# Throwaway products, a permuted identity, first-column steps and a new hand-written order in a fused FFT and state-space kernel

## The chip, the cores and the metric

The kernel runs on one core of one Trainium2 chip. The core has five engines that run their own instruction queues side by side: TensorE (PE in the profile, with its weight loads as PEld), VectorE (DVE), ScalarE (ACT), GpSimd (POOL) and SyncE (SP, which only starts transfers here). The metric is the device time in microseconds (us) of one execution, lower is better. The kernel before takes 306.85 us, the median of three runs that lie between 306.59 and 307.20 us.

## The reference

Two long computations on the same input x of 2048 tokens by 1024 channels (bf16) are blended by a gate:

```python
x = A_x
g = _sigmoid((x * gate_w).sum(-1, keepdims=True))
a = irfft2(rfft2(x) * (w_r + 1j * w_i))            # over tokens and channels
# b: a diagonal complex recurrence over the tokens
Lam_bar = exp(dt * Lam);  B_bar = ((Lam_bar - 1) / Lam)[:, None] * Bmat
Bu = einsum("bld,pd->blp", x, B_bar)
h = Lam_bar * h + Bu[:, t]                          # for t in 2048 tokens
b = 2 * einsum("blp,dp->bld", hseq, Cmat).real + x * Dskip
return g * a + (1 - g) * b
```

## The kernel before

**Spectral half.** Both directions of the two-dimensional transform are matrix products with constant tables. The 2048 tokens are taken as 16 groups j of 128. `turn` (L932) transposes a group on TensorE by eight products of 128 columns with the permuted identity `ident_g`, and `turn_out` (L941) copies the result to `xQ`; groups 12 to 15 come transposed by DMA. `fold` (L951) makes even and odd parts on VectorE, for the last groups with a mirrored half (`mirror`, `fold_odd`). `fd` (L432) is the first transform on TensorE, `fd_out` (L458) evicts it on ScalarE, `s1` and `s1_out` (L466, L478) are the first half of the token transform, which is stored to DRAM. `s2` (L602) is the second half, `times_w` (L628) multiplies by the weights on VectorE (tile `UV`), `is1`, `is2` (L640, L673) and `spectral_mm` (L819) go back.

**First column.** Column 0 of the spectrum packs two real columns and has its own small chain, `middle` (L533): a reversal of a weight tile (`Wrev`), a combination on GpSimd (`Wh`, `AB`), a small transform (`Bcol`, `Zp`), its reversal (`Zr`), a complex product (`Q`, `Qb`) and a permutation (`qps`, `Qn`). Its small TensorE products stand in the one TensorE queue between large ones; `Qn` overwrites column 0 of the tile `X2` before `times_w` reads it, and `unit_cols` (L623) sets column 0 of the weights to one.

**State-space half.** The tokens are eight chunks c of 256. `unit_mm` (L403) makes four blocks of 32 products (tile `psu`) for each chunk, which needs all 16 groups of `xQ` and the DMA-transposed matrix `BT`. `unit_out` (L414) evicts them on ScalarE to `h`. `recur` (L329) runs the recurrence as a list of small VectorE and ScalarE steps ("pieces"): products with tables `tab`, a scan (L368), joins. `early_mm` and `own_mm` (L751, L885) multiply `h` with the matrix C, 16 products for half a token tile (`ps_y`, `ps_q`). The tables come from `make_tab` (L274): an angle for each of eight blocks (L280 to L283), its sine and cosine, and products with them. `turn_vectors` (L1094) and `small` (L1147) make the vectors that these need.

**The start.** GpSimd makes `ident` (L216); VectorE permutes it to `ident_g` (L218) and clears a tile `idle` (L1000, shown as `A`); `keep_warm` (L1002) multiplies that tile with itself WARM times, into a buffer that nobody reads (`psw`). FILL_T and FILL_V add transposes of `ident` that are overwritten at once (L936, L1099). On SyncE the loads of x, the tables G and T2, and B follow each other.

**The order.** Tile scheduling is off. The string ORDER (L58) is the program: each letter runs the next step of one generator in `acts` (L1190), and each engine gets its instructions in that order and executes them in that order. T is a turn, U its copy, f a step of `fold`, F `fd`, E its eviction, S and A `s1` and its eviction, 1 its store, V and a the vectors, t a step of `make_tab`, x, G, 2, b, c, k, M and W loads, h and H `unit_mm` and its eviction, v the next piece of PIECES, s a step of `middle`, j of `unit_cols`, n and N `early_mm` and its scaling, J and + the store and the accumulating store, 3 to 8 the way from `s2` to the store of `is1`, i and I `is2` and its eviction. SLOTS hands the four PSUM buffers out in a fixed sequence, and CLOSES is the order of the finished tiles.

## Time and profile before

The profiled execution took 306.91 us by the device's clock; its span, from the first to the last recorded instruction or transfer, is 305.1 us.

| what | before |
|---|---|
| median of 3 runs | 306.85 us (306.59 to 307.20) |
| profiled execution, time and span | 306.91 us, 305.1 us |
| TensorE | 294.8 us busy, 97% of the span |
| VectorE | 289.2 us, 95% |
| ScalarE | 207.0 us, 68% |
| GpSimd | 72.0 us, 24% |
| moved by DMA | 59.21 MB, mean 194 GB/s |

A profile row names start and length in us, engine, line of the kernel, operation, written and read tile, shape and count; a bracket gives the idle time of the engine ahead of it and what ended it. A time window's row gives the window, then each engine's busy time with its instructions, the clock granted to TensorE, the share of the DMA engines and GB/s. A chain row gives start, length, engine, tile and line of one link of the work that ended last. A group's row ends in busy time, mean length in ns of one instruction, and idle time ahead of it. Matmuls are pipelined: their recorded lengths overlap, so the pace is the distance between starts.

### The profile page before, as it was taken

How to read it: one execution, taken by the hardware profiler on the slowest of the kernel's cores; microseconds unless marked ns; L12 is line 12 of the kernel's file. 1: busy time of each engine (PE TensorE's matmuls, PEld its weight loads, DVE VectorE, ACT ScalarE, POOL GpSimd, SP SyncE). 2: the span in 40 equal slices, each digit the busy share in tenths (PEclk: the TensorE clock that was granted, in tenths of full speed). 3: DMA queues.
4: the chain of work that ended last, by engine and by line, in shares of the span. 5: the costliest groups of instructions: out<-in, count | busy, mean ns of one | idle time of the engine just before them, and what ended most of it. 6: DMA issues, size and time to landing. Idle time of an engine off the chain costs nothing.

```text
span 305.1 us, 6248 instructions
## 1 busy us (share of the span) xinstructions
PE 294.8 (97%) x2464; PEld 195.4 (64%) x2464; DVE 289.2 (95%) x374; ACT 207.0 (68%) x309; POOL 72.0 (24%) x106
## 2 busy tenths in 40 slices
PE   7989999999999999999999999999999999999993
PEld 4555687886884584467564763688567995465442
DVE  3999999999989999999999999999999999999993
ACT  1699999897541385958886888856979866393200
POOL 1133155393710002110202112120102033351430
PEclk9999999999999999999999999999999999999999
DMA  7999996999994977899989868998659726999796
GB/s 236 367 210 195 202 227 190 105 208 154 217 247 82 259 174 145 201 261 280 212 220 216 213 163 206 236 245 248 179 167 210 145 26 124 156 175 187 104 142 227
DMA packets 74140, 59.21 MB, mean 194 GB/s; under 512 B 44872, under 2 KB 61664, under 8 KB 74112
## 3 DMA queue, kind: packets, MB, share of 16 engines
q1 hardware_dynamic: 66560, 49.69, 64.6%
q0 software_dynamic: 6896, 8.69, 23.2%
q10 hardware_dynamic: 656, 0.44, 0.4%
q8 instruction: 19, 0.31, 0.4%
q14 instruction: 9, 0.07, 0.1%
HBM read 27.33 MB, written 23.08 MB: 165 GB/s over the span
## 4 chain that ended last, share of the span: by engine, by line
PE 68%; DVE 21%; ACT 5%; issue 3%; DMA 2%; POOL 0%; SPq 0%; POOLq 0%; ACTq 0%; DVEq 0%
PE ps_y L732 24%; PE psu L410 23%; PE ps_q L746 7%; DVE h L368 3%; DVE h L343 2%; PE ps_id L829 2%; DVE xQ L947 2%; DMA xs<-in_A_x_dram 2%; DVE UV L632 1%; ACT ZT L690 1%; PE ps_is L681 1%; PE ps_id L825 1%; PE ps_s L474 1%; PE ps_fd L455 1%; PE ps_s L609 1%
## 5 line engine op out<-in xcount | busy, mean ns | idle before, releaser
L410 PE MATMUL psu<-xQ,BT 128*128 128x256 bf16 x1024 | 115.7, 273 | 0.4 <-ACT A_last L489 0.3
L410 PEld LDWEIGHTS <-BT 128*128 128x128 bf16 x1024 | 99.3, 98 | 16.4 <-issue 3.8
L732 PE MATMUL ps_y<-CT,h 128*128 128x512 bf16 x416 | 93.5, 379 | 0.7 <-ACT ye L763 0.4
L732 PEld LDWEIGHTS <-h 128*128 128x128 bf16 x416 | 39.8, 98 | 48.8 <-issue 3.9
L804 POOL DMA_DIRECT2D y_scratch<-su x20 | 17.8, 953 | 127.3 <-ACT su L798 95.3
L420 ACT CAST h<-psu 128x1024 bf16<-128x1024 f32 x32 | 32.1, 1013 | 17.4 <-PE psu L410 12.5
L343 DVE TENSOR_TENSOR h<-h,tab 128x4096 bf16<-128x4096 bf16 (+1 forms) x20 | 37.3, 1863 | 0.6
L368 DVE TENSOR_TENSOR_SCAN h<-rz,h 128x512 bf16<-128x512 f32 (+1 forms) x14 | 36.3, 2617 | 0.2
L763 ACT ACTIVATE ye<-ps_y,omg 128x512 f32<-128x512 f32 x26 | 17.4, 686 | 17.6 <-PE ps_y L732 9.9
L372 ACT ACTIVATE xQ<-h,r_sb 128x254 bf16<-128x254 bf16 x48 | 21.3, 503 | 9.1 <-DVE h L368 9.1
L340 DVE TENSOR_TENSOR xQ<-h,tab 128x4096 bf16<-128x4096 bf16 x12 | 27.4, 2281 | 0.0
L746 PE MATMUL ps_q<-CT,h 128*128 128x512 bf16 (+2 forms) x112 | 20.9, 349 | 0.0
L870 POOL DMA_DIRECT2D BT<-y_scratch x10 | 12.6, 1538 | 27.4 <-issue 23.3
L619 ACT CAST X<-ps_s 128x1024 bf16<-128x1024 f32 x16 | 16.1, 1007 | 4.3 <-PE ps_s L609 2.9
L690 ACT CAST ZT<-ps_is 128x1024 bf16<-128x1024 f32 x16 | 16.9, 1113 | 2.0 <-issue 1.2
L656 ACT CAST C<-ps_is 128x1024 bf16<-128x1024 f32 x16 | 15.6, 1010 | 3.4 <-PE ps_is L648 2.6
L836 ACT ACTIVATE BT<-ps_id,gB 128x1024 bf16<-128x1024 f32 x14 | 15.1, 1111 | 3.6 <-DMA out_dram<-BT 1.8
L746 PEld LDWEIGHTS <-h 128*128 128x128 bf16 x112 | 10.4, 98 | 10.5
L461 ACT CAST X<-ps_fd 128x1024 bf16<-128x1024 f32 x16 | 16.1, 1015 | 0.1
L798 ACT ACTIVATE su<-xs,omg 128x512 f32<-128x512 bf16 x20 | 14.0, 720 | 0.5 <-DVE xs L788 0.5
L372 ACT ACTIVATE su<-h,r_sb 128x254 bf16<-128x254 bf16 x16 | 7.0, 495 | 8.4 <-DVE Zp L572 4.6
L947 DVE COPY xQ<-pt 128x1024 bf16<-128x1024 bf16 x12 | 8.1, 682 | 3.8 <-PE pt L938 3.8
(211 smaller groups left out, 432.9 us busy)
## 6 DMA issues: line engine op xcount, KB each, us to landing
y_scratch<-ye SPq DMA_DIRECT2D x20, 256.0 KB, 2.9
y_scratch<-su POOLq DMA_DIRECT2D x20, 256.0 KB, 6.5
Bb<-turn_scratch SPq DMA_DIRECT2D x16, 256.0 KB, 4.8
turn_scratch<-C SPq DMA_DIRECT2D x16, 256.0 KB, 4.3
raw<-turn_scratch SPq DMA_DIRECT2D x8, 512.0 KB, 5.2
xs<-in_A_x_dram SPq DMA_DIRECT2D x13, 256.0 KB, 5.3
out_dram<-BT SPq DMA_DIRECT2D x11, 256.0 KB, 4.8
CT<-in_A_x_dram SPq DMA_DIRECT2D x5, 512.0 KB, 5.2
```

What stands on the lines that cost most here:

```text
L340: nc.vector.tensor_mul(out=tmps["s"], in0=u[:, :, ::-1], in1=bc(i))
L343: nc.vector.tensor_mul(out=u, in0=u, in1=bc(i))
L368: nc.vector.tensor_tensor_scan(out=seg, data0=flat(rz, i), data1=seg, initial=0.0, op0=ALU.mult, op1=ALU.add)
L372: nc.scalar.activation(out=tmps["s"][:, 0, :, i, 1:TS], in_=u[:, 1, :, i, 0:TS - 1], func=ACT.Copy, scale=r2_sb[:, js.start + i:js.start + ...
L410: nc.tensor.matmul(psu[:, j, :], lhsT=BT[4 * q + j][:, ri, d8, :], rhs=xQ[:, c, d8, :], start=(d8 == 0), stop=(d8 == 7))
L420: nc.scalar.copy(out=hs[c][:, :, ri, 4 * q:4 * q + 4].rearrange("p e b (q j) -> p e b q j", j=16), in_=psus.pop((c, q, ri)).rearrange("p b ...
L461: (nc.vector.tensor_copy if j in FD_DVE else nc.scalar.copy)(out=X1.rearrange("p r (m e c) -> p r m e c", e=2, c=2), in_=psf.pop(j).rearra ...
L690: nc.scalar.copy(out=fft["ZT"][:, kp, :, :, 2 * G:2 * G + 2], in_=pszs.pop((G, kp)).rearrange("p v (x n) -> p x n v", n=64))
L732: nc.tensor.matmul(psy, lhsT=hs[c][:, tq, ri, jb, :], rhs=CT[ri][:, jb, 512 * dh:512 * (dh + 1)], start=(i == 0), stop=(i == 15 and tb not ...
L746: nc.tensor.matmul(psq, lhsT=hs[c][:, tq, ri, jb, :], rhs=CT[ri][:, jb, at:at + n], start=(i == 0), stop=(i == 15))
L763: nc.scalar.activation(out=ye, in_=psys[tb][:, K * hf:K * (hf + 1)], func=ACT.Copy, scale=omg[:, tb:tb + 1])
L804: nc.gpsimd.dma_start(out=y_dram[tb, hf], in_=xgs[tb, hf], accum_op=ALU.add)
```

## The change

WARM goes from 7 to 5. FILL_T gives turn 2 six throwaway transposes where it had 22. `ident_g` is copied by GpSimd. All eight angles are made by ScalarE, where four were made by VectorE. In `middle`, the five copies and one negation that VectorE did (`Wrev`, `Bcol` twice, `Zp`, `Zr`, `Qn`) go to ScalarE, and the five steps of the complex product (`Q`, `Qb`) go to GpSimd, as do the four small copies of `unit_cols`. PIECES, SLOTS and ORDER are new; the steps in them are the same steps.

```diff
@@ -34,38 +34,38 @@
 NTURN = 12
 
 FILL_V = (0, 0, 4)
-FILL_T = {2: 22}
-WARM = 7
+FILL_T = {2: 6}
+WARM = 5
 FD_DVE = ()
-ANG_ACT = (4, 5, 6, 7)
+ANG_ACT = (0,1,2,3,4,5,6,7,)
 S1_DVE = ()
 TURN_DVE = tuple(range(16))
 CLOSES = (0, 1, 2, 3, 10, 4, 5, 11, 12, 6, 7, 8, 9)
 PIECES = (
-    0, 1, 3, 2, 4, 5, 6, 7, 9, 8, 10, 11, 12, 13, 14, 15, 16, 17, 18, 20, 21, 19, 22, 24, 23, 25, 26, 27, 28, 29, 30,
-    31, 32, 33, 34, 35, 36, 37, 38, 40, 39, 41, 42, 43, 45, 44, 46, 47, 48, 62, 49, 50, 51, 52, 63, 53, 56, 65, 64,
-    54, 66, 55, 57, 58, 67, 59, 61, 60, 68, 69, 71, 74, 80, 81, 72, 73, 82, 83, 75, 70, 84, 76, 77, 79, 78, 85, 86,
-    87, 90, 89, 98, 99, 91, 101, 92, 93, 100, 88, 94, 95, 96, 102, 103, 97, 104, 105, 108, 116, 106, 107, 117, 110,
-    119, 118, 109, 111, 120, 121, 112, 113, 122, 123, 114, 115, 125, 126, 124, 127, 128, 134, 135, 136, 137, 129, 138,
-    139, 140, 141, 146, 130, 131, 133, 144, 145, 143, 147, 142, 148, 149, 150, 151, 132, 152, 153, 154, 155, 156, 157,
-    158, 159, 160, 163, 162, 161, 164, 165, 166, 168, 167,
+    0, 1, 2, 3, 5, 4, 6, 9, 7, 8, 10, 11, 12, 14, 13, 15, 16, 17, 18, 20, 21, 22, 23, 19, 24, 25, 26, 27, 28, 29, 30,
+    31, 33, 32, 34, 35, 36, 37, 38, 40, 39, 41, 42, 43, 45, 44, 46, 47, 48, 49, 50, 51, 52, 62, 53, 56, 55, 63, 64,
+    54, 57, 65, 66, 58, 67, 68, 59, 69, 61, 60, 70, 80, 74, 81, 73, 71, 72, 83, 75, 82, 84, 85, 86, 76, 77, 79, 78,
+    87, 88, 92, 98, 99, 101, 91, 100, 90, 89, 93, 102, 94, 95, 96, 97, 103, 104, 105, 109, 110, 116, 107, 106, 117,
+    108, 119, 118, 111, 120, 112, 113, 121, 115, 114, 122, 123, 128, 134, 135, 124, 137, 125, 126, 136, 127, 138, 139,
+    140, 129, 141, 145, 130, 131, 144, 142, 143, 146, 147, 133, 148, 149, 151, 150, 132, 152, 153, 155, 154, 156, 157,
+    158, 159, 162, 163, 161, 160, 164, 165, 166, 168, 167,
 )
...
 MIRROR = (6, 7, 8, 9)
 ORDER = (
-    "xTUffxxVVTTUGaTffGV2VVVG|far|xaFEUffFfUttxaTTfFSTktxx2TfEUUfttUAfUSAEaTwFEffafTrtfttStUFFEfUtTffbFEA",
-    "fSUf~uF2TUEbttxxUUSArU1EASSUAAtSFEFbbbbbttbAtffget~frbEutttbbhHtbftttS1FEbffbtttbAb~tt1t1ut11hHSvAFE",
-    "ftvhH~urrrr1tFF1vStKcEeScccctckf11AvvEtvccvvtthhthvhttthttvcHttetttcct1tAHHHtvvvcfeHFEvwvvvvvSvtvtSv",
-    "ttvvvvvvFvvvwvvcccvvvvvvEwcA11hSSA1AK1hAe1KKKKsYsYshsHsHsHhhvvvvvvvMLnWHvvvnvNJnvvvsNJnvvvvssvsvMMvv",
-    "sshsvNvYsHLyyNs3hs44vvvvHhWHMvmm+j5535M44MJnMW6nnH3Mvvvm7v7N5vJvv+vn5WvM4N8856hvhvJm4vvJ7vWY+Wvj5H3N",
-    "J7vN5H44h56y8v+j8m+YHhM377H8v54ymWn84556vNndvvvhJMvv5M3M5N77nn+5dvhvvvvYy6hvvvv8m+vm445WHJJNNmdM37Mh",
-    "87vHJH558+mv44j6v8YMy77n83YX+mJHNnJ8+vv554+y4m56vN5nvY5v5hv768yv7vNvmnvv877v+mvvJHhJH8+8vqhvvYiivmhq",
-    "qiii+yvmNIIvqniYHHvIvii+IvIIvvvvvIqJqnqiIvIiIvvm+mNNJJvvvvvnviIivi%nI+vNvvvvvIyvqiIhXYNiivvHIhIlHJlp",
-    "phlzJzlZXZPPzzhZZZZHRRHRRRRppZZZZdmyPZo+ROvZvlQQlQoooDzvDmOvvPlQBvvRvBzZZZv++vpOBDDYlOvoZPZZQRRQvRRR",
-    "zzRBDvZpPloOlCZDzovZZZOvZoYDzvBBvooYYQZZoZZRZRDQZ9RooDQRRyR9C00yDDD9C99Q09900D00",
+    "xTxTUfffVV2UVVxTVGVaatffUfGtGTFxtaxxEt2FTffUfTTSxxxFETTUUttUAffffSbEaSAAUkFT|EfUbbfaa|ftrFfFUTSrEEAf",
+    "fUfSATUwftttbFb~uFUUUEES1UtAttStbbFShbtttAAFfEffrrtttrf~Htfuhttt2~fuEtgtttbHvtbbbbetSFFEtAvbhE1tttbS",
+    "ASvvbttf1F1hvvKtHh~vrttffttE11ttehwv1r1t1hvtHuSvvvFvtvFvttccFtttt1cerHHhvtvccccwvAAEKvv1HEESSvvchcvv",
+    "tvttScv1wAvAKHe11AKvcSvvKkvvvA11KvvesHhvvsccHnvvccchMhsvvhvvvHLWsvvvvvWWsnssHsMNvvvnvsnsvvvvNvvYssYv",
+    "JNJNHhJjWsvvsHsshMMLvYvvvv3vyvh3jvv44Hm+n5M55H4m6y+nvv457MM73JmvhnvvMMY556NNvnh44v8v3v8m7JNJNv8v+YWW",
+    "v+hymh578Mv+H55v6ymYv4vnHmJ+Hv455+Jm+v773vjMMHvY4458Whvv6Nvv8nnvv3vny77vNM5hvmJ4HN+4WM556vvvJNMv88mM",
+    "hd773H54n55y688+JJH4mXjY7+Nhvv7dmH38nJY54455v6yvv5vvv8m78N5v5vvvvJn+h67N877+nvvyhh8mv8qNqiihiiqHHHYq",
+    "vim+mYvIJ+nivivIiHIJIIqqvyvvvvqvnvIIiiIvvNNvni+XvyiJmI+vmIIIivvvvvInvvJX+vivIYyvqvdNvvhNiIivh%IllHHv",
+    "pphzzZZmPPllzzHZZZZQhRRvoRJRRRpZZllQRdRZ+ZHvZZQvOvBDQDzzvJDDoOBDlpPPZZlZooovvZllvZRRZvQzmYzOOvRRpQRB",
+    "vvovBZZRoZPZCv+ZZOOBBDDovzzvZYZvvZZQQZpPZRRRyoooDRRQY9D90oRoCy990C99Q9DDD0D0000Y",
 )
 
 EVEN = ((0, 0), (2, 1), (2, 0), (0, 1))
@@ -215,7 +215,7 @@
     ident = cpool.tile([P, P], BF16, name="ident")
     make_identity(nc, ident)
     ident_g = cpool.tile([P, P], BF16, name="ident_g")
-    nc.vector.tensor_copy(out=ident_g.rearrange("p (g s) -> p g s", g=2), in_=ident.rearrange("p (s g) -> p g s", g=2))
+    nc.gpsimd.tensor_copy(out=ident_g.rearrange("p (g s) -> p g s", g=2), in_=ident.rearrange("p (s g) -> p g s", g=2))
     chpi = cpool.tile([P, 1], FP32, name="chpi")
     nc.vector.memset(chpi, HALF_PI)
     tau_i = tmp.tile([P, TC], I32, name="tau_i")
@@ -544,7 +544,7 @@
         wrps = reverse_m(Wc, 4, "Wrev")
         yield
         Wrev = fx.tile([P, 16, 4], FP32, name="Wrev")
-        nc.vector.tensor_copy(out=Wrev, in_=wrps)
+        nc.scalar.copy(out=Wrev, in_=wrps)
         yield
         Wh = fx.tile([P, 16, 4], FP32, name="Wh")
         nc.gpsimd.tensor_add(out=Wh[:, :, 0:4:2], in0=Wc[:, :, 0:4:2], in1=Wrev[:, :, 0:4:2])
@@ -559,8 +559,8 @@
         nc.tensor.transpose(out=aps, in_=Acol.rearrange("p g j -> p (g j)"), identity=ident)
         yield
         Bcol = fx.tile([32, 3, 4, 16], BF16, name="Bcol")
-        nc.vector.tensor_copy(out=Bcol[:, 0:2], in_=aps.rearrange("j (r b a) -> j r a b", r=2, a=4))
-        nc.vector.tensor_scalar_mul(out=Bcol[:, 2], in0=Bcol[:, 0], scalar1=-1.0)
+        nc.scalar.copy(out=Bcol[:, 0:2], in_=aps.rearrange("j (r b a) -> j r a b", r=2, a=4))
+        nc.scalar.activation(out=Bcol[:, 2], in_=Bcol[:, 0], func=ACT.Copy, scale=-1.0)
         yield
         zps = psum([P, 2, 16], "zps")
         Kc_sb, Ks_sb = fft["K3"][:, 0], fft["K3"][:, 1]
@@ -569,7 +569,7 @@
                              start=(i == 0), stop=(i == 7))
         yield
         Zp = fx.tile([P, 16, 2], BF16, name="Zp")
-        nc.vector.tensor_copy(out=Zp, in_=zps.rearrange("p c b -> p b c"))
+        nc.scalar.copy(out=Zp, in_=zps.rearrange("p c b -> p b c"))
         yield
         zrp = reverse_m(Zp, 2, "Zrev")
         yield
@@ -579,22 +579,22 @@
         Q = fx.tile([P, 2, 2, 2, 16], FP32, name="Q")
         each = lambda t: t.unsqueeze(2).to_broadcast([P, 2, 2, 16])
         every = lambda t: t.unsqueeze(1).to_broadcast([P, 2, 2, 16])
-        nc.vector.tensor_copy(out=Zr[:, 0], in_=zrp[:, :, 0])
-        yield
-        nc.vector.tensor_mul(out=Q[:, 0], in0=each(AB[:, 0]), in1=every(Zp.rearrange("p b r -> p r b")))
-        yield
-        nc.vector.tensor_mul(out=Q[:, 1], in0=each(AB[:, 1]), in1=every(Zr))
-        nc.vector.tensor_add(out=Q[:, 0], in0=Q[:, 0], in1=Q[:, 1])
+        nc.scalar.copy(out=Zr[:, 0], in_=zrp[:, :, 0])
+        yield
+        nc.gpsimd.tensor_mul(out=Q[:, 0], in0=each(AB[:, 0]), in1=every(Zp.rearrange("p b r -> p r b")))
+        yield
+        nc.gpsimd.tensor_mul(out=Q[:, 1], in0=each(AB[:, 1]), in1=every(Zr))
+        nc.gpsimd.tensor_add(out=Q[:, 0], in0=Q[:, 0], in1=Q[:, 1])
         yield
         Qb = fx.tile([P, 16, 2], BF16, name="Qb")
-        nc.vector.tensor_sub(out=Qb[:, :, 0], in0=Q[:, 0, 0, 0], in1=Q[:, 0, 1, 1])
-        nc.vector.tensor_add(out=Qb[:, :, 1], in0=Q[:, 0, 1, 0], in1=Q[:, 0, 0, 1])
+        nc.gpsimd.tensor_sub(out=Qb[:, :, 0], in0=Q[:, 0, 0, 0], in1=Q[:, 0, 1, 1])
+        nc.gpsimd.tensor_add(out=Qb[:, :, 1], in0=Q[:, 0, 1, 0], in1=Q[:, 0, 0, 1])
         yield
         qps = psum([P, 32], "qps")
         nc.tensor.matmul(qps, lhsT=KRS_sb[:, 2, :], rhs=Qb.rearrange("p b r -> p (b r)"), start=True, stop=True)
         yield
         Qn = fft["Qn"] = fx.tile([P, 16, 2], BF16, name="Qn")
-        nc.vector.tensor_copy(out=Qn.rearrange("p b r -> p (b r)"), in_=qps)
+        nc.scalar.copy(out=Qn.rearrange("p b r -> p (b r)"), in_=qps)
         yield
 
     ps2s, X2s, UVs, pscs, C1s, pszs = {}, {}, {}, {}, {}, {}
@@ -622,7 +622,7 @@
 
     def unit_cols():
         for p in range(4):
-            nc.vector.tensor_copy(out=fft["Wb"][p % 2][:, :, :, 0], in_=unit_w.unsqueeze(2).to_broadcast([P, 2, 4]))
+            nc.gpsimd.tensor_copy(out=fft["Wb"][p % 2][:, :, :, 0], in_=unit_w.unsqueeze(2).to_broadcast([P, 2, 4]))
             yield
 
     def times_w():
```

More of the change, by code (lines that the diff above doesn't have):

```diff
@@ L44 @@
 PIECES = (
[7 rows of a table removed]
[7 rows of a table added]
 )
 SLOTS = (
-    "0123012320132012012310210321032103201230132013201302310231012312032103131201203103203013031203120312",
-    "0312310210321021321032320310321032032031031023102310210321230120310321032",
+    "0123013203102310230123102310321032130231023012032023013021321021302330313021321032132013103201231201",
+    "2123203103201301301320201320132013013201201231203120320131320312003121032",
 )
```

## The prediction

> **What bounds the kernel now.** I read the page's busy shares first, then time windows cut at the places where the chain of waits changes its engine, then the chain in order of time, then the rows around each place.
>
> ```profile
> PE 294.8 (97%) x2464; PEld 195.4 (64%) x2464; DVE 289.2 (95%) x374; ACT 207.0 (68%) x309; POOL 72.0 (24%) x106
> 5.65:20.85 15.20, 13.59 (x147) 9.16 (x145) 14.99 (x51) 10.44 (x20) 2.39 (x11) 1.00 1.09 309
> 33.79:90.69 56.90, 56.22 (x503) 46.69 (x502) 53.82 (x84) 46.09 (x67) 28.79 (x46) 1.00 1.05 190
> 90.69:210.00 119.31, 118.88 (x1013) 73.69 (x1011) 117.94 (x109) 81.82 (x131) 13.09 (x15) 1.00 0.86 211
> 210.00:240.00 30.00, 29.11 (x254) 20.02 (x253) 29.47 (x22) 26.75 (x40) 2.62 (x3) 1.00 0.82 198
> ```
>
> Two engines are nearly full. In the first of these windows VectorE is busy for 14.99 of 15.20 us and TensorE is not (13.59): the start belongs to VectorE. Later TensorE leaves holes of 0.68, 0.43 and 0.89 us in the last three windows, 2.0 us in all. So the end comes when TensorE's work is done: it counts when TensorE becomes continuous, how much work it then has, and which holes stay.
>
> ```profile
> 0.72 0.20 POOL masks.py:197 MEMSET ident<- 128x128 bf16 x1 [0.29 <-POOLq L1223]
> 1.33 0.35 DVE ident_g L218
> 1.68 0.17 DVE A L1000
> 1.90 3.17 PE psw L1005 x7
> 5.65 0.70 DVE xQ L947
> 279.57 20.77 PE ps_q L746 x112
> 300.37 0.35 DVE raw L918
> out_dram<-raw ACTq DMA_DIRECT2D x1, 32.0 KB, 3.1
> ```
>
> In the chain, VectorE first waits for GpSimd's identity, only then clears the tile (L1000) for the seven products, and only behind these do the turns start. VectorE carries the chain from 5.65 on through that first window, TensorE's last stretch ends at 300.3, and a short VectorE step and a store of 3.1 us follow. The tail is the same in the new order, so I leave it.
>
> **The change part by part.**
>
> *The start.* Without the copy, VectorE's first instruction waits for nothing. GpSimd's work on the identity starts at 0.72, and the clearing takes some 0.3 us: the products can start at about 1.1 in place of 1.9.
>
> ```profile
> 0.73 1.35 SPq L247 DMA_DIRECT2D CT<-in_A_x_dram  x3
> CT<-in_A_x_dram SPq DMA_DIRECT2D x2, 256.0 KB, 2.8
> 4.86 0.76 PE L938 MATMUL pt<-ident_g,CT 128*128 128x128 bf16 x8
> 6.12 0.62 PE L938 MATMUL pt<-ident_g,CT 128*128 128x128 bf16 x8
> L1058 POOL COPY Wp<-CT 128x64 bf16<-128x64 bf16 x1 | 0.2, 238 | 4.8 <-DMA CT<-in_A_x_dram 4.8
> L1072 POOL COPY Wc<-Wp 128x32 bf16<-128x32 bf16 x1 | 1.0, 1025 | 4.0 <-DMA Wp<-in_A_w_i_dram 4.0
> ```
>
> Seven products last from 1.90 to 4.86, 0.42 us each; five from 1.1 end at 3.2. The first x lands 2.8 us after 0.73, at 3.5: this now ends the wait, at 3.5 against 4.86. The first turn's pace shows the clock: its eight took 0.14 us longer than the next eight. Wholly at the slow pace it takes about 1.1 us, so VectorE's first copy starts at about 4.6 against 5.65, 1.05 earlier. GpSimd's permuted copy lies between 0.24 us (128x64 at L1058) and 4.1 us (four times the 1.025 us of the 128x32 copy at L1072, by elements); I take 0.4, since no VectorE copy runs beside it then. Up to 2.1 us it is hidden behind the load.
>
> *To the first `psu`.* That product needs all 16 copies to `xQ`.
>
> ```profile
> 12.36 0.53 DVE ang L283 x2
> 28.93 0.87 DVE L306 SCALAR_TENSOR_TENSOR tab<-sc,cr,t 128x256 bf16<-128x256 f32 x2
> 29.72 1.42 DVE L947 COPY xQ<-CT 128x1024 bf16<-128x1024 bf16 x4
> 31.06 0.87 DVE L306 SCALAR_TENSOR_TENSOR tab<-sc,cr,t 128x256 bf16<-128x256 f32 x2
> 6.57 1.39 PE L936 MATMUL pt<-ident 128*128 128x128 bf16 x22
> 30.75 0.38 PE L442 MATMUL ps_fd<-G_sb,preT 128*128 128x128 bf16 x2
> 33.79 0.38 PE L410 MATMUL psu<-xQ,BT 128*128 128x256 bf16 x2
> L281 ACT ACTIVATE ang<-tau_f,ang 128x256 f32<-128x256 f32 x4 | 1.8, 502 | 0.0
> ```
>
> Before, VectorE has the last copy done at 31.1. The new order takes two angles (0.53 us) out of that stretch and puts two table steps (0.8 us) behind it: 31.1 - 1.05 - 0.53 - 0.8 = 28.7. The `fd` ahead of it needs the mirrored fold that stands just ahead of the last four copies (1.35 us), at 27.4; with `fd` (some 1.0 us) and one `s1` (some 0.55) TensorE reaches `psu` at about 29.0. The old order has a second `fd`, the gate and a mirror between 30.75 and 33.79; the new one puts these 3.04 us behind the first `psu`. Like for like that is 29.0 against 30.75: **1.75 us earlier**; I take 1.65 for the new wait of `s1` for its eviction. The 16 missing fillers (16 of 22 in 1.23 us from start to start, 0.9 us) are part of it. TensorE then idles some 3 us ahead of `psu`, so the fillers' time is mostly idle time: their cover is VectorE. On SyncE the small first part of T2 passes the second x block, JP falls behind the DMA transposes of x, and the first B loads move behind those; each only delays what is needed later than it lands. Further on, weight loads pass the first x tiles and early stores, which by the order are needed 5 us and more of TensorE work later; nothing for them. The four angles cost ScalarE 4 x 0.50 us; it is idle for 32% of the span, and in this stretch their results are asked for about 1 us after it can have them. Without that margin VectorE would wait for them, up to the 1 us of two angles.
>
> *The later holes.* VectorE also loses the other two angles, the four copies of `unit_cols` and eleven column steps of about 0.2 us each, some 3 us in all.
>
> ```profile
> 212.12 1.21 DVE L387 TENSOR_TENSOR h<-h,xQ 128x2048 bf16<-128x2048 bf16 x1
> 212.37 0.61 PE L681 MATMUL ps_is<-KRS_sb,raw 128*128 128x128 bf16 x8 [0.39 <-ACT h L420]
> 213.39 2.58 PEld L732 LDWEIGHTS <-h 128*128 128x128 bf16 x13 [0.53 <-DVE h L387]
> 75.48 0.61 PE L474 MATMUL ps_s<-X,raw 64*128 64x512 bf16 x4 [0.30 <-ACT A_last L489]
> ```
>
> At 213 TensorE waits for the last join of chunk 4 (L387). In the new order that join stands some 10 us of VectorE work further ahead of the same product, so this hole should close; what is late next is ScalarE, which evicts for `is2`. At 75 it is ScalarE that is late, and it gets more to do. I take **1.0 of the 2.0 us** of holes as saved, between 0 and 2.0.
>
> *Column steps on GpSimd.* TensorE's queue has the permutation product (`qps`) behind large blocks; a late `Qb` holds everything behind it.
>
> ```profile
> L586 DVE TENSOR_TENSOR Q<-AB,Zr 128x64 f32<-128x64 f32 x1 | 0.2, 216 | 0.0
> 101.50 3.56 PE ps_y L732 x16
> 105.10 3.50 PE psu L410 x32
> 71.93 1.70 ACT su L372 x4
> 78.27 1.23 DVE L340 TENSOR_TENSOR su<-h,tab 128x2048 bf16<-128x2048 bf16 x1
> 78.41 1.16 POOL L1035 TENSOR_SCALAR omg_bf<-g_bf 128x16 bf16<-128x16 bf16 x1
> 86.29 0.25 POOL L551 TENSOR_TENSOR Wh<-Wc,Wrev 128x32 f32<-128x32 bf16 x1
> 23.34 1.99 POOL L270 COPY rz<-r_sb 128x256 f32<-128x256 f32 x1
> 25.43 0.40 POOL L270 COPY rz<-r_sb 128x256 f32<-128x256 f32 x1
> ```
>
> Five steps go from 0.22 us on VectorE (L586) to GpSimd. Before, only one block of `psu` stands between the reversal and `qps`; in the new order a block of `ps_y` and one of `psu` do, some 7.0 us. Two `next_` steps (1.70), one scaling (some 0.7) and small copies on ScalarE take 3.0 of it, so the four GpSimd steps behind them have 4.0 us, **1.0 us each**.
>
> A small GpSimd step takes 0.25 us where VectorE rests (86.3), another 1.16 us beside a VectorE product, ending 0.07 us after it; one copy took 1.99 us where its twin took 0.40. Beside the recurrence I take 1.16: four make 4.64, so `qps` waits **0.6 to 0.7 us**. The ends are 0.25 (no wait) and 1.99 (4.0 us). The Trainium skill (SBUF — State Buffer, "SBUF: two separate sides") says that VectorE and GpSimd take one pair of ports as an exclusive lock and the loser blocks for the whole instruction; these rows agree. By the page's rule the move is not free even of a fast step, and a step that loses the lock several times gives the third rival below; with no lock this term would be nothing.
>
> `unit_cols` on GpSimd is queued among the accumulating stores (L804), which wait for ScalarE and for transfers; its columns are needed 10 us and more of VectorE work later, so I take nothing. ScalarE's `Bcol` copy now stands ahead of the last eviction of chunk 2 and waits for a product two blocks later; VectorE arrives there at about the same time, so between 0 and 1 us of VectorE's slack go, which TensorE does not see.
>
> *Sum.* 306.91 - 1.65 - 1.0 + 0.6 = 304.86 us for the profiled execution, which lies 0.06 above the median: **304.8 us**.
>
> **The rivals.** *More holes close*: the start gains 0.4 more, all 2.0 us of holes go and `qps` doesn't wait: 306.91 - 2.05 - 2.0 = 302.9. For it: VectorE loses some 4 us in all and starts earlier. Against: ScalarE gets 2.9 us more. *The loads hold the start*: the second x block lands later, now that part of T2 passes it, and later blocks as before, so only the fillers' 0.9 us is gained, with 0.4 of the holes: 306.91 - 1.3 + 0.6 = 306.2. For it: the DMA share of 1.09 in that window, which is full. Against: VectorE shows no wait for a load there. *GpSimd loses the ports*, the slower side: four steps at 1.99 us make `qps` 4.0 us late, and TensorE with it: 306.91 - 2.65 + 4.0 = 308.3. It is slower than before from a mean step of 1.0 + 2.65/4 = 1.66 us on. For it: the row of 1.99 us; against: the others at 1.2 and below. *The clock comes late*: five products are 2.1 us of work. If the turns behind them didn't keep TensorE busy enough, each us at half pace would cost about 0.4 us of the path (half, less the 10% of holes in that window): granted at 13 us in place of 5, that is 3.2 us: 308. It decides at about 10 us; against it stands that the turns follow without a gap. The Trainium skill (TensorE: Matmul & The Clock Gate, "Part 1: The HAM clock gate") says that full clock follows a window of about 3.4 us of sustained work, and that the window runs free of the kernel's start. By that rule a late window here ends before 8 us, which costs nothing; the trace agrees in that the pace changes about 3.2 us after the first product.
>
> **How the numbers follow.** The forecast has 0.52, more holes 0.12, loads 0.16, ports 0.14, late clock 0.06. What a measurement can tell from no change is 0.2%, 0.6 us. Faster by more: 0.52 + 0.12 + 0.06 of the loads (whose time lies at the bound) = 0.70; same: 0.10 of the loads and 0.03 of the clock = 0.13; slower: 0.14 + 0.03 = 0.17. The forecast's own range is 303.4 to 306.1 (holes from 0 to 2.0, `qps` from 0 to 1). The range that holds 8 in 10 reaches half into the first rival and past the second: 302.5 to 307.0.
>
> **What would show it.** Right: the first product near 1.1, the first turn near 3.5, VectorE's first copy near 4.6, the first `psu` near 29.0, no hole at the product of chunk 4, GpSimd's `Q` steps near 1.2 us and a hole below 1 us ahead of `qps`. Wrong: a first `psu` later than 30.5, `Q` steps near 2 us, slow-paced turns after 8 us, or new holes of more than 1 us where TensorE waits for VectorE or for ScalarE's `Bcol`.

## The result and the profile after

The changed kernel takes 302.44 us (median of 4 runs, 301.95 to 304.53) against 306.94 us (4 runs, 306.59 to 307.20): a ratio of 0.9867, 95% interval 0.982 to 0.9914. The profiled executions take 302.45 and 306.91 us, 4.46 us apart, and the spans are 300.7 and 305.1 us. The changed kernel's execution of 304.53 us has a mean granted clock of 0.992; the other three have 0.999 or 1.0 and lie between 301.95 and 302.45 us.

From the page of the changed kernel, the line of busy times:

```profile
PE 293.6 (98%) x2446; PEld 194.7 (65%) x2446; DVE 286.6 (95%) x354; ACT 208.6 (69%) x319; POOL 88.4 (29%) x116
```

The four time windows that were cut for the kernel before, at the same clock times, of the changed kernel (columns as before):

```profile
5.65:20.85 15.20, 13.44 (x129) 8.92 (x130) 14.93 (x49) 12.29 (x23) 3.94 (x11) 1.00 1.08 291
33.79:90.69 56.90, 56.59 (x508) 44.72 (x506) 53.59 (x81) 44.16 (x66) 32.12 (x46) 1.00 1.12 193
90.69:210.00 119.31, 118.80 (x1024) 74.59 (x1023) 118.28 (x98) 83.45 (x136) 24.45 (x23) 1.00 0.87 214
210.00:240.00 30.00, 30.00 (x277) 21.51 (x275) 29.26 (x23) 29.05 (x43) 3.49 (x4) 1.00 0.82 196
```

VectorE is busy 2.6 us less and GpSimd 16.4 us more, with ten small steps added to it. The start still belongs to VectorE (14.93 of 15.20 us). Of TensorE's holes in the last three windows 0.31, 0.51 and nothing are left, 0.82 us of 2.0, and the one of 0.89 us is gone. The rest of the answer is in rows. From the timeline of the changed kernel, the start:

```profile
1.36 0.29 POOL L218 COPY ident_g<-ident 128x128 bf16<-128x128 bf16 x1
1.21 2.31 PE L1005 MATMUL psw<-A 128*128 128x512 bf16 x5 [1.21 <-DVE A L1000]
3.62 1.89 PE L938 MATMUL pt<-ident_g,CT 128*128 128x128 bf16 x16
4.69 0.69 DVE L947 COPY xQ<-pt 128x1024 bf16<-128x1024 bf16 x1 [3.54 <-PE pt L938]
7.16 1.07 PE L938 MATMUL pt<-ident_g,CT 128*128 128x128 bf16 x16 [0.40 <-DMA CT<-in_A_x_dram]
9.76 0.28 DVE L966 TENSOR_TENSOR preT<-sums 128x256 bf16<-128x256 bf16 x1
15.48 0.58 DVE L966 TENSOR_TENSOR preT<-sums 128x256 bf16<-128x256 bf16 x1
27.64 0.69 DVE L995 TENSOR_TENSOR preT<-preT,ps_r 128x512 bf16<-128x512 bf16 x1
29.91 3.67 PE L410 MATMUL psu<-xQ,BT 128*128 128x256 bf16 x32
```

And the end, from the same timeline: the last VectorE step, and SyncE's stores of 256 KB:

```profile
297.54 0.35 DVE L918 SCALAR_TENSOR_TENSOR raw<-ps_q,omg,xQ 128x128 bf16<-128x128 f32 x1 [0.28 <-PE ps_q L746]
290.85 3.44 SPq L878 DMA_DIRECT2D out_dram<-BT  x4
```

The changed kernel's DMA issues from 284 us on, the last store (the last number is the time to landing in us, 3.1 before):

```profile
out_dram<-raw ACTq DMA_DIRECT2D x1, 32.0 KB, 1.5
```

The timeline of the kernel before, the same stores on SyncE:

```profile
294.96 2.62 SPq L878 DMA_DIRECT2D out_dram<-BT  x3
299.47 0.33 SPq L878 DMA_DIRECT2D out_dram<-BT  x1
```

I split each span at two marks: the first `psu`, and the end of VectorE's last step. The new order puts 3.04 us of TensorE work behind the first `psu` that stood ahead of it, so for a kernel in the old order the first mark is taken 3.04 us earlier (30.75 in place of 33.79), as in the prediction. The three parts sum to the span.

| profiled execution | to first `psu` | to VectorE's end | to the span's end |
|---|---|---|---|
| before | 30.75 | 269.97 | 4.38 |
| after | 29.91 | 267.98 | 2.81 |
| difference | -0.84 | -1.99 | -1.57 |

The middle part as time windows, from the first mark to the start of VectorE's last step, of the kernel before and then of the changed one:

```profile
30.75:300.37 269.62, 267.59 (x2227) 178.91 (x2224) 263.60 (x300) 185.57 (x277) 63.95 (x82) 1.00 0.88 188
29.91:297.54 267.63, 266.78 (x2227) 178.62 (x2225) 261.15 (x283) 186.05 (x284) 79.61 (x91) 1.00 0.92 193
```

TensorE runs the same 2227 products in both. Its idle time there falls from 2.03 to 0.85 us, which is 1.18 of the 1.99; the other 0.81 is time that counts as busy. Most of that lies in `is2` (L681), whose products had waited several times in the kernel before and don't wait now: 0.5 us less idle time, and from start to start, idle time left out, 0.9 us less. A product of 0.22 us recorded length at a pace of 0.06 covers up to 0.16 us of the wait behind it, so holes read from busy time come out too small.

The prediction had -1.65, -0.4 (holes -1.0, `qps` +0.6) and 0: none of these three parts has the measured size.

### The profile page after: what moved, and what is told of

Its sections match the earlier page's. It is cut to its first block, busy times and chain, and to the rows that moved or that the text cites. A ratio compares the mean times of both kernels' runs of the same rounds, so it can differ in the third digit from the quotient of the medians.

```text
span 300.7 us, 6230 instructions
## 1 busy us (share of the span) xinstructions
PE 293.6 (98%) x2446; PEld 194.7 (65%) x2446; DVE 286.6 (95%) x354; ACT 208.6 (69%) x319; POOL 88.4 (29%) x116
## 4 chain that ended last, share of the span: by engine, by line
PE 69%; DVE 21%; ACT 4%; DMA 3%; issue 1%; DVEq 0%; ACTq 0%
PE ps_y L732 29%; PE psu L410 23%; PE ps_q L746 7%; DVE xQ L947 3%; DMA y_scratch<-su 2%; PE ps_is L681 2%; PE ps_id L829 2%; DVE tab L306 2%; DVE preT L961 2%; DVE sums L963 2%; DVE h L368 2%; PE ps_is L648 1%; DVE su L340 1%; DVE h L343 1%; PE ps_id L825 1%
## 5 line engine op out<-in xcount | busy, mean ns | idle before, releaser
L804 POOL DMA_DIRECT2D y_scratch<-su x20 | 19.2, 979 | 96.9 <-ACT su L798 70.9
L340 DVE TENSOR_TENSOR xQ<-h,tab 128x4096 bf16<-128x4096 bf16 x12 | 27.4, 2284 | 0.5 <-ACT h L420 0.5
L870 POOL DMA_DIRECT2D BT<-y_scratch x10 | 13.8, 1637 | 30.3 <-issue 26.0
L372 ACT ACTIVATE xQ<-h,r_sb 128x254 bf16<-128x254 bf16 x48 | 20.4, 506 | 0.0
L300 POOL TENSOR_SCALAR tab<-sc,rinv 128x256 bf16<-128x256 f32 x8 | 11.4, 1426 | 6.3 <-ACT sc L295 6.1
```

The source lines that it names most:

```text
L340: nc.vector.tensor_mul(out=tmps["s"], in0=u[:, :, ::-1], in1=bc(i))
L372: nc.scalar.activation(out=tmps["s"][:, 0, :, i, 1:TS], in_=u[:, 1, :, i, 0:TS - 1], func=ACT.Copy, scale=r2_sb[:, js.start + i:js.start + ...
L804: nc.gpsimd.dma_start(out=y_dram[tb, hf], in_=xgs[tb, hf], accum_op=ALU.add)
```

## The experiments

Medians are of all runs of a kernel; ratios are to the kernel before on the same chip (its medians there were 306.88, 307.06 and 306.51 us), with 95% intervals. The three parts are those of the profiled execution, which differs from the median by up to 1 us.

| kernel | median us | ratio | to `psu` | to VectorE's end | to the end |
|---|---|---|---|---|---|
| new order alone | 308.57 | 1.0054 (1.0039 to 1.0069) | 31.81 | 272.01 | 2.78 |
| moves alone, old order | 309.65 | 1.0089 (1.0072 to 1.0105) | 31.10 | 272.76 | 4.04 |
| the same, unit columns on VectorE | 306.98 | 1.0000 (0.9985 to 1.0014) | 30.13 | 270.37 | 3.70 |
| before, new tail | 306.51 | 0.9985 (0.9971 to 0.9998) | 30.77 | 270.37 | 3.16 |
| after, tile 9 stored later | 302.80 | 0.9872 (0.9852 to 0.9892) | 29.89 | 267.58 | 2.83 |
| after, tile 9 stored last | 303.42 | 0.9882 (0.9864 to 0.9901) | 29.98 | 268.29 | 3.33 |
| after, column steps on VectorE | 306.32 | 0.9985 (0.9973 to 0.9996) | 30.15 | 271.62 | 2.83 |
| after, three `Q` steps doubled | 307.13 | 0.9987 (0.9965 to 1.0008) | 29.74 | 272.90 | 2.76 |
| after, old start | 303.77 | 0.9903 (0.9884 to 0.9921) | 31.16 | 268.37 | 2.77 |
| after, four angles on VectorE | 303.94 | 0.9911 (0.9895 to 0.9927) | 30.60 | 269.49 | 2.81 |
| after, 22 fillers | 302.21 | 0.9864 (0.9846 to 0.9881) | 30.77 | 267.90 | 2.83 |
| after, T2 behind G | 302.34 | 0.9861 (0.9846 to 0.9877) | 29.91 | 267.96 | 2.83 |

### The order alone, and the moves alone

The strings are the same length in letters and steps in both kernels, so each can be run with the other's. The first run is the kernel before with these three tables replaced:

```diff
-PIECES, SLOTS, ORDER = (those of before)
+PIECES, SLOTS, ORDER = (those of after)
```

> The kernel before with the new order, pieces and slots alone: seven products, 22 fillers, the permuted identity, the column steps and the first four angles stay as they were. Theory A (three separate places: start -0.8, holes -2.0, tail -1.6 us; the tail is a matter of the order, the start of the moves, the holes of both): 304.0 to 304.8 us, with the last store landing in about 1.5 us as in the changed kernel, and TensorE's first psu at or after 30.7. Rival B (the moves off VectorE carry the whole gain, the order only fits to them): 306.3 to 307.3, or slower, with holes of over 1 us where TensorE waits for VectorE. Rival C (the order carries it all): 302.2 to 302.9.

The second is the changed kernel with the tables of before:

```diff
-PIECES, SLOTS, ORDER = (those of after)
+PIECES, SLOTS, ORDER = (those of before)
```

> The changed kernel with the order, pieces and slots of the kernel before: five products, 6 fillers, identity, angles and column steps as changed. Theory A: the start gains about 1 us, the holes that wait for VectorE part of their 2.0, the tail nothing (last store still about 3 us): 304.6 to 305.6. Rival B (the moves carry it): 302.2 to 303.2. Rival C (the order carries it): 306.5 to 307.3.

None of the theories holds for both runs. A and C fall with the first, which rival B fits (slower, with a wait of 1.2 us for VectorE), and B falls with the second. The order alone is 1.7 us slower than before, the moves alone 2.8 us slower, and both together 4.5 us faster: against the sum of the two the pair brings about 9 us. The tables of waits show where (total, times and longest in us). First the order alone, VectorE's and then TensorE's waits between 85 and 130 us:

```profile
DVE Zp L572 <- PE zps L568: 2.5, 1, 2.5
PE psu L410 <- ACT ye L763: 1.8, 1, 1.8
PE ps_is L648 <- DVE UV L635: 1.2, 1, 1.2
```

In the new order the small product `zps` stands behind a block of `ps_y`. With `Zp` still on VectorE, VectorE stands 2.5 us in line for it in the middle of the recurrence. That delays its scan, the scan delays ScalarE's next steps, so `ye` leaves its PSUM buffer late, and TensorE waits; VectorE stays late, and the first `ps_is` waits for `UV`.

The moves in the old order, VectorE's waits between 85 and 130 us and in the first 36 us:

```profile
DVE UV L632 <- POOL Wb L625: 3.9, 1, 3.9
DVE rot_kk L1129 <- ACT ang L281: 2.2, 2, 1.3
```

GpSimd's timeline in the same kernel, just ahead of the first of these waits' end:

```profile
115.73 0.95 POOL L804 DMA_DIRECT2D y_scratch<-su  x1 [6.36 <-ACT su L798]
116.39 0.52 POOL L625 COPY Wb<-unit_w 128x8 bf16<-128x8 bf16 x1
```

Here GpSimd has a copy of 0.52 us for VectorE (`unit_cols`), behind an accumulating store that waits 6.36 us for ScalarE, and VectorE stands 3.9 us. At the start VectorE also waits 2.2 us for the angles, since the old order asks for them before ScalarE has them. The time window from 210 to 240 us (TensorE's busy time is the second number), in the run with the order alone:

```profile
210.00:240.00 30.00, 29.84 (x273) 21.40 (x274) 29.50 (x22) 28.22 (x43) 3.48 (x4) 1.00 0.95 242
```

The same window in the run with the moves alone:

```profile
210.00:240.00 30.00, 28.95 (x257) 20.10 (x258) 29.50 (x20) 26.55 (x39) 2.62 (x3) 1.00 0.79 193
```

The hole at chunk 4 is closed by the order (29.84 of 30.00 busy without any move) and not by the relief of VectorE (28.95 with all of it).

### What one moved part is worth in each order

The changed kernel with the steps of `middle` back on VectorE, `unit_cols` left on GpSimd:

```diff
-        nc.scalar.copy(out=Zp, in_=zps.rearrange("p c b -> p b c"))
+        nc.vector.tensor_copy(out=Zp, in_=zps.rearrange("p c b -> p b c"))
...
-        nc.gpsimd.tensor_mul(out=Q[:, 0], in0=each(AB[:, 0]), in1=every(Zp.rearrange("p b r -> p r b")))
+        nc.vector.tensor_mul(out=Q[:, 0], in0=each(AB[:, 0]), in1=every(Zp.rearrange("p b r -> p r b")))
...
```

> The changed kernel with the eleven first-column steps back on VectorE, their places in the order kept (angles, unit columns, identity, products and fillers stay as changed). Theory E (what the move is worth is not VectorE's 2 to 3 us of busy time but its standing in line: on VectorE the copy of Zp waits 2.4 us for a product behind a block of ps_y, and the Q chain, in VectorE's order behind large steps, makes the permutation product late): VectorE idle for 2 to 3 us between 90 and 120 us, TensorE holes of 1 to 2 us ahead of psu3.1.0 and of the first ps_is; 305.0 to 306.7 us. Rival F (it is VectorE's busy time alone, and TensorE sets the end): 302.4 to 303.2 us, no hole over 0.5 us there.

306.32 us, 3.9 us more than the changed kernel: the first theory. From the timeline, VectorE, ScalarE and TensorE in turn:

```profile
97.09 0.19 DVE L572 CAST Zp<-zps 128x32 bf16<-128x32 f32 x1 [2.44 <-PE zps L568]
103.61 1.70 ACT L372 ACTIVATE su<-h,r_sb 128x254 bf16<-128x254 bf16 x4 [2.74 <-DVE h L368]
105.93 3.65 PE L410 MATMUL psu<-xQ,BT 128*128 128x256 bf16 x32 [1.82 <-ACT ye L763]
123.18 0.93 PE L648 MATMUL ps_is<-UV,raw 32*64 32x512 bf16 x16 [1.23 <-DVE UV L635]
```

The wait is handed on from row to row: 2.44 us of VectorE, 2.74 of ScalarE, 1.82 and 1.23 of TensorE, none of which VectorE or TensorE has there in the changed kernel. Eleven steps of about 0.2 us have some 2.2 us of work; it is the standing in line that costs. So in this order nearly the whole gain hangs on moves that the prediction priced as a loss.

The old order with all moves but one:

```diff
-            nc.gpsimd.tensor_copy(out=fft["Wb"][p % 2][:, :, :, 0], in_=unit_w.unsqueeze(2).to_broadcast([P, 2, 4]))
+            nc.vector.tensor_copy(out=fft["Wb"][p % 2][:, :, :, 0], in_=unit_w.unsqueeze(2).to_broadcast([P, 2, 4]))
```

> The run with all moves in the old order (309.65 us), with the four unit columns alone back on VectorE. Theory E (there VectorE waited 3.9 us for a unit column that GpSimd's queue held behind an accumulating store, which waited 6.4 us for ScalarE): that wait goes, and with it the holes of 2.1 us that TensorE had between 124 and 136 us: 307.0 to 307.9 us. Rival F (the wait only covered another one): 309.0 to 310.2.

306.98 us, 2.7 us less than with that copy on GpSimd: four copies of some 0.2 us were worth nearly all that the moves alone had lost. What is left of the moves in the old order is then no gain at all (ratio 1.0000).

### The room ahead of the permutation product

The changed kernel's rows there, GpSimd and then TensorE:

```profile
102.78 1.18 POOL L586 TENSOR_TENSOR Q<-AB,Zr 128x64 f32<-128x64 f32 x1 [3.54 <-ACT Zr L582]
104.03 0.73 POOL L587 TENSOR_TENSOR Q<-Q 128x64 f32<-128x64 f32 x1
104.85 1.09 POOL L590 TENSOR_TENSOR Qb<-Q 128x16 bf16<-128x16 f32 x1
105.89 0.26 POOL L591 TENSOR_TENSOR Qb<-Q 128x16 bf16<-128x16 f32 x1
103.53 3.66 PE L410 MATMUL psu<-xQ,BT 128*128 128x256 bf16 x32
107.03 0.18 PE L594 MATMUL qps<-Qb,KRS_sb 128*128 128x32 bf16 x1
107.06 3.65 PE L410 MATMUL psu<-xQ,BT 128*128 128x256 bf16 x32
```

From the start of the first step to the product there are 4.25 us, near the 4.0 that were forecast. The four steps take 3.26 us, 0.82 in the mean and not 1.16, and are done 0.88 us ahead of the product, which waits for nothing. Three of the steps are doubled, writing the same values twice:

```diff
         nc.gpsimd.tensor_mul(out=Q[:, 1], in0=each(AB[:, 1]), in1=every(Zr))
+        nc.gpsimd.tensor_mul(out=Q[:, 1], in0=each(AB[:, 1]), in1=every(Zr))
...
         nc.gpsimd.tensor_sub(out=Qb[:, :, 0], in0=Q[:, 0, 0, 0], in1=Q[:, 0, 1, 1])
+        nc.gpsimd.tensor_sub(out=Qb[:, :, 0], in0=Q[:, 0, 0, 0], in1=Q[:, 0, 1, 1])
...
```

> The changed kernel with three of GpSimd's column steps issued twice (the second Q product and both Qb steps, the same values written again). In the changed kernel the last Qb step ends about 0.9 us ahead of its product. Theory E (GpSimd has 0.9 us to spare there, and a step beside VectorE costs 0.3 to 1.2 us): three more steps of 1.9 to 3.0 us in all make the product 1.0 to 2.1 us late, a hole of that size ahead of psu3.1.0, and 303.2 to 304.5 us in the end. Rival F (room of several us): no hole, 302.2 to 302.8.

307.13 us, 4.7 more, beyond the expected range. From the timeline of this run (its lines stand three later than before), TensorE:

```profile
109.76 0.18 PE L597 MATMUL qps<-Qb,KRS_sb 128*128 128x32 bf16 x1 [2.75 <-POOL Qb L594]
109.79 5.32 PE L410 MATMUL psu<-xQ,BT 128*128 128x256 bf16 x32
```

Three time windows of the same run, with TensorE's busy time behind the length and the granted clock third from the right:

```profile
107.00:109.70 2.70, 0.01 (x1) 0.00 (x0) 2.67 (x5) 1.01 (x1) 2.54 (x4) 1.00 0.94 251
111.00:112.00 1.00, 1.00 (x7) 0.69 (x6) 1.00 (x1) 0.00 (x0) 1.00 (x1) 0.50 0.90 259
114.00:115.00 1.00, 1.00 (x11) 0.74 (x8) 1.00 (x2) 0.00 (x0) 0.00 (x0) 1.00 0.00 0
```

The room is as small as the theory says: the product now waits 2.75 us. What the theory missed is that the hole takes the clock with it. The next block of `psu` takes 5.32 us in place of 3.65, at a granted clock of 0.50 until it is back at 1.00 ahead of 114. That is 1.67 us more, 4.4 with the wait. It doesn't happen each time: seven of the twelve executions have a mean granted clock of 0.987 to 0.994 and take 307.0 to 307.9 us (the profiled one is among them, 0.993), five have 0.999 or 1.0 and take 304.8 to 306.3. The medians of the two groups are 1.8 us apart. So by the second group, of which no trace is kept, the hole alone costs some 3.2 us, still beyond the expected range, since the product is later than was expected (2.75 us, not 1.0 to 2.1).

### The start

The changed kernel with seven products, 22 fillers and the permuted identity on VectorE:

```diff
-FILL_T = {2: 6}
-WARM = 5
+FILL_T = {2: 22}
+WARM = 7
...
-    nc.gpsimd.tensor_copy(out=ident_g.rearrange("p (g s) -> p g s", g=2), in_=ident.rearrange("p (s g) -> p g s", g=2))
+    nc.vector.tensor_copy(out=ident_g.rearrange("p (g s) -> p g s", g=2), in_=ident.rearrange("p (s g) -> p g s", g=2))
```

> The changed kernel with seven products, 22 fillers and the permuted identity on VectorE; angles, column steps and order stay. Theory G (VectorE's start carries the first psu one for one): VectorE's first copy at 5.9 in place of 4.69, first psu 0.9 to 1.4 us later, 303.3 to 304.0 us. Rival H (the first block of the order is held by the loads of x and G, so the early start is mostly waited away): first psu at most 0.4 us later, 302.3 to 302.9.

303.77 us, 1.3 more, and the first `psu` 1.25 us later, as the first theory has it. The four angles alone:

```diff
-ANG_ACT = (0,1,2,3,4,5,6,7,)
+ANG_ACT = (4, 5, 6, 7)
```

> The changed kernel with the first four angles back on VectorE, in their places in the order. Theory G (VectorE is the bound up to the first psu; two angles of 0.27 us stand in that stretch, two behind it): first psu 0.4 to 0.6 us later, 302.8 to 303.2 us. Rival L (the angles' step to ScalarE is worth more, since ScalarE takes them beside other work while VectorE would stand in line for them): over 303.3. Rival H (something else holds the first psu): 302.2 to 302.6.

303.94 us, 1.5 more: the rival by its number, though the first `psu` is only 0.69 us later, which is near the first theory. The rest comes behind it: the part up to VectorE's end is 1.51 us longer, in an execution of 304.66 us, the longest of this kernel's six. Two waits of TensorE behind the first `psu` are new in it, from the table of waits:

```profile
PE ps_is L681 <- DMA raw<-turn_scratch: 0.5, 1, 0.5
PE zps_g L1019 <- DVE preT L995: 0.3, 1, 0.3
```

The second, at 39 us, is for a fold of VectorE; whether the angles have to do with the first, a load at 207 us, stays open. The fillers alone, and the load order alone:

```diff
-FILL_T = {2: 6}
+FILL_T = {2: 22}
```

> The changed kernel with 22 fillers at the third turn, as before. Theory G (the fillers stand in TensorE's wait for the x block and for G, VectorE has its next tile in time): first psu within 0.2 us of 29.91, 302.2 to 302.8 us. Rival M (fillers and products count alike, 0.9 us of TensorE work at the start reach the end): 303.1 to 303.5.

```diff
-"xTxTUfffVV2UVVxTVGVaatffUfGtGTF..."
+"xTxTUfffVVUVVxTVGVaatffUfGtG2TF..."
```

> The changed kernel with the first small part of T2 loaded behind the three parts of G and the next x block, not ahead of them. Theory G (TensorE's waits of 0.7 and 0.9 us for G at 8 to 9 us stand beside VectorE's work, which is the bound): the wait for G shrinks by about 0.4 us, the first psu stays within 0.3 us, 302.1 to 302.7 us. Rival H (the loads hold the start): first psu 0.4 to 0.8 us earlier, 301.6 to 302.0, which would beat the changed kernel.

The fillers change nothing in the median (302.21 against 302.44), nor does T2's place (302.34): there TensorE's wait for G is gone, one for x has grown to 0.9 us, and the first `psu` stands at 29.91 as before. In the profiled execution with 22 fillers, the longest of its five, the first `psu` came at 30.77, but a load was late in it too. TensorE's wait for G there, from the table of waits:

```profile
PE ps_fd L455 <- DMA G_sb<-c_G: 1.3, 1, 1.3
```

The same row of the changed kernel:

```profile
PE ps_fd L455 <- DMA G_sb<-c_G: 0.7, 1, 0.7
```

So of the start's parts the products with the identity count 1.3 us, the angles 0.7 us up to the first `psu`, and the fillers nothing. Put on the order alone, 31.81 - 1.25 - 0.69 = 29.87 against 29.91 measured: here the parts add up, closer than single executions allow (five kernels with the whole changed start reach the first `psu` between 29.74 and 30.15). The order itself costs 1.06 us (31.81 against 30.75).

### The tail

The kernel before with the last acts laid as in the changed one (the letters of PE stay in their sequence):

```diff
-"...ZZoZZRZRDQZ9RooDQRRyR9C00yDDD9C99Q09900D00"
+"...ZZoZZZZRRRyDQRRQ9D90oRoCy990C99Q9DDD0D0000"
```

> The kernel before, with the non-TensorE letters of the last 40 acts alone laid as in the changed kernel: the spectral steps of tiles 8 and 9 ahead of those of tile 15, the accumulating loads of tiles 7 to 9 earlier, the second product of tile 13 stored earlier, and the 256 KB store of tile 9 ahead of the last small stores. Theory A (the last small store lands late because it collides with the 256 KB stores): 305.1 to 305.8 us, the last store landing in 1.5 to 2.0 us after its issue. Rival D (the tail got shorter because VectorE reaches it earlier, the order there is nothing): 306.6 to 307.2, last store at 3 us.

The changed kernel with the 256 KB store of tile 9 two places later, and then behind everything:

```diff
-"...DDD0D0000Y"
+"...DDD000D00Y"
```

> The changed kernel with one act moved: the 256 KB store of tile 9 goes behind the second and third last stores of SyncE's and ScalarE's queues, as in the kernel before. Theory A: the last 32 KB store again meets it, and lands 0.8 to 1.6 us later: 303.2 to 304.0. Rival D (the place of that store is nothing, only VectorE's earlier arrival counts): 302.2 to 302.7.

```diff
-"...DDD0D0000Y"
+"...DDD00000DY"
```

> The changed kernel with the 256 KB store of tile 9 put behind all the last stores (one act moved). Theory J (the tail of the kernel before was long because that store, queued behind a store that waited for VectorE's last steps, was issued 1.3 us before VectorE's end; where it was issued that late, the end came 5.5 us after its issue, the transfer's own length and no collision): issue at about 297.6, end of the span 5 to 5.7 us later, 2 to 2.6 us later than now: 304.4 to 305.1 us. Rival K (the length of the tail comes from the accumulating loads and the other stores): 302.2 to 302.9.

The last column of the table settles one thing. All eight profiled executions that keep the new order and its tail end 2.76 to 2.83 us behind VectorE, whatever else is changed in them; those in the old order take 3.70 to 4.38. So the 1.57 us come from the order. Giving the kernel before the new tail brings 1.22 us of it (3.16), and its last store lands in 1.8 us, as theory A has it, though the median moves by 0.4 only, between both expectations. The store of tile 9 alone is not the cause that I took it for. Two places later it was still issued 2.8 us ahead of VectorE's last step, and nothing changed. Issued last, it costs 0.5 us of the tail and not 2 to 2.6 (the median rose by 1.0, and the profiled execution lost 0.4 ahead of the tail as well). Nor did it take the 5.5 us of theory J in the kernel before. There it landed 3.8 us after its issue, as the DMA issues around 299.5 us show:

```profile
out_dram<-BT SPq DMA_DIRECT2D x1, 256.0 KB, 3.8
```

What sets the tail is the last store of 32 KB. In all fourteen profiled executions the span ends 1.28 or 1.29 us behind its landing. What the DMA engines moved between its issue and its landing, before and then after:

```profile
DMA packets 632, 0.56 MB, mean 182 GB/s; under 512 B 207, under 2 KB 511, under 8 KB 632
DMA packets 288, 0.13 MB, mean 89 GB/s; under 512 B 160, under 2 KB 288, under 8 KB 288
```

It landed 3.1 us after its issue with 0.56 MB on the way, and 1.5 us with 0.13. The kernels between them keep nearly this sequence: 1.8 us with 0.27 MB (new tail), 2.0 with 0.39 (tile 9 last), 2.4 with 0.37 and 2.7 with 0.53 (old order, with the moves). In the kernel before all of the 0.56 MB is on the queues of SyncE's and ScalarE's stores, none on the queue of the accumulating loads. So the last store is slow beside the stores that are still under way, the 256 KB ones and the smaller ones together, and no accumulating load runs beside it. Which of these stores counts how much, and whether the loads had held them up earlier, stays open.

## Why the prediction was right or wrong

- **The total** has the forecast's direction, but the gain is twice the forecast's. It lies 2.4 us below its value and at the lower end of its range: 0.06 us below by the medians, and just inside by the ratio (0.9867 of 306.85 us is 302.8). Three parts were off the same way by 1.57, 1.0 and 0.6 us, one by 0.8 us the other way. That the range nearly holds the time is luck in part: the start, counted 0.8 us too large, makes up for half of the tail, which was put at nothing. The ends of the forecast's own range, 303.4 and 306.1, come out of its terms as 303.2 and 306.2.
- **"VectorE's first copy starts at about 4.6 against 5.65"**: right. Products at 1.21 (forecast 1.1), identity 0.29 us (0.4), copy at 4.69.
- **"TensorE reaches `psu` at about 29.0"**: mis-sized, 29.91. VectorE lost the work that was counted, but its last fold is done at 28.33 and not at 27.4. From its first copy to its last, the steps of the same shapes on L963, L966, L968 and L971 take 0.8 us more in sum, start to start, with steps of GpSimd beside some of them: L966 takes 0.58 us at 15.48, beside two of these, and 0.28 at 9.76, beside none. Other steps beside GpSimd were no longer than usual, and no run tests it, so the cause is read from the rows and not shown. The step left it out: it priced GpSimd's slowdown beside VectorE, and none of VectorE beside GpSimd.
- **"The 16 missing fillers ... are part of it ... mostly idle time"**: the second half was right, and the fillers count nothing.
- **"Without that margin VectorE would wait for them, up to the 1 us of two angles"**: the margin is there in the new order; without it VectorE waits 2.2 us.
- **The holes, "1.0 of the 2.0 us"**: near by the idle time that it counted, 1.18. The stretch got 1.99 shorter, since waits that were recorded as busy time went too (0.81). The hole at chunk 4 closed for the reason given, the join's place in the order. The changed kernel keeps 0.85 us, 0.7 of it in two waits for ScalarE's `h`.
- **"`qps` waits 0.6 to 0.7 us"**: didn't occur. The room was right (4.25 for 4.0), the steps were shorter (0.82 for 1.16). The graver fault is the term beside it: what the column steps free on VectorE was counted as "some 3 us in all" of busy time, with no term of its own in the sum. Undone in the new order they cost 3.9 us, since VectorE then waits in line for TensorE's small products, which this order has put behind large blocks. The prediction asked of the moved steps what waits behind them on the new engine, and never what would wait behind them on the old one in the new order.
- **"`unit_cols` ... I take nothing"**: right in this order; in the other one the same move costs 2.7 us by the very queue that the step names.
- **"The tail is the same in the new order, so I leave it"**: the step that failed outright. The chain ahead of it ends in one VectorE step and one store of 3.1 us, and what else was under way beside that store was not looked at. The new order lays those transfers differently, the same store takes 1.5 us, and the tail is 1.57 us shorter.
- **The rivals.** "More holes close" came nearest by its number (302.9), and `qps` indeed didn't wait. But 0.85 us of holes stayed, the start gained less and not more, and what makes up for these is the tail, which it doesn't have: the number is luck. "GpSimd loses the ports" has a real place: with steps doubled the kernel is back at the time of before, and the price per us is higher than was worked out, since a long hole can also halve the clock. "The loads hold the start" shows at most in one execution in the old order, where the third x block ended a wait of 1.67 us; in the new order the first `psu` stayed when T2's place was changed. "The clock comes late" didn't happen: 16 products of the turns take 1.89 us from 3.62 on and 1.07 from 7.16 on, so the full pace was there ahead of 8 us.

## What to carry to other kernels

A small step on an in-order engine is worth the time for which its wait blocks what stands behind it, not its own 0.2 us; ask this of the engine it leaves as well as of the one it goes to. Edits of engine and of order are one change: priced or tried one at a time, each of these two would have been thrown away as a loss. And follow the last transfers to their landing, since the end of compute is not the end of the kernel.

## What the hardware showed besides

**A hole of 2.75 us can drop TensorE's clock.** After it the granted clock was 0.50 for about 3.4 us (1.67 us lost at half pace). By the mean granted clocks it did so in seven of twelve executions: 3.4 us at half pace in some 300 us give a mean of 0.994, and those seven have 0.987 to 0.994. Where the longest hole was 1.82 us (the order alone, and the column steps on VectorE) the clock was 1.00 in every window that I read, and one of 18 executions has a mean of that size. One of the changed kernel's four has it too (0.992); which holes that one had isn't known, so a long hole need not be the only way to it. The Trainium skill (TensorE: Matmul & The Clock Gate, "Part 1: The HAM clock gate") has the throttle return after an idle window of about 3.4 us; here less than that did it, and the measurement decides.

**A copy of 128x8 on GpSimd took 4.13 us beside a scan.** From the timeline of the changed kernel, GpSimd and VectorE:

```profile
109.98 4.13 POOL L625 COPY raw<-unit_w 128x8 bf16<-128x8 bf16 x1 [3.83 <-DMA raw<-in_A_w_i_dram]
109.68 4.42 DVE L368 TENSOR_TENSOR_SCAN h<-rz,h 128x2048 bf16<-128x2048 f32 x1
```

The same copy in the timeline of the kernel with the column steps on VectorE:

```profile
112.40 0.41 POOL L625 COPY raw<-unit_w 128x8 bf16<-128x8 bf16 x1 [14.44 <-DMA raw<-in_A_w_i_dram]
```

It starts 0.3 us into the scan and ends 0.01 us after it; at another moment it takes a tenth. The Trainium skill (SBUF — State Buffer, "SBUF: two separate sides") says that the loser of the ports blocks for the whole instruction, and these rows agree. Six other kernels in the new order have the same copy beside the same scan, for 3.96 to 4.36 us, ending 0.01 us after it each time; in the one with 22 fillers it began just ahead of the scan and took 0.22 us. Its column is needed at 115.9 at the earliest, so nothing waits. Had one of the four `Q` steps fallen beside a scan of this length, the room of 0.88 us would have been gone.

**The same start differs by about 1 us from run to run.** The two kernels in the old order, with all moves and with all but the unit columns, have the same program up to the first `psu`, and reach it at 34.14 and 33.17. The turn of the third x block in the timeline of the first, with all moves:

```profile
8.09 1.07 PE L938 MATMUL pt<-ident_g,CT 128*128 128x128 bf16 x16 [1.67 <-DMA CT<-in_A_x_dram]
```

The same row of the second, with the unit columns on VectorE:

```profile
6.78 1.07 PE L938 MATMUL pt<-ident_g,CT 128*128 128x128 bf16 x16 [0.82 <-DMA CT<-in_A_x_dram]
```

So a single profiled execution hardly tells half a microsecond at the start.
